# Two spectral layers and two Mish MLPs on one core: the transposed turn through memory, one pipeline step fewer, the ordered filter kept early

## The chip, the cores and the metric

One core of one Trainium2 chip runs the whole program in one launch. The metric is device time in microseconds (us). The kernel before took 1103.34 us, the median of three runs (1102.86 to 1104.55). The profile comes from one further execution of it.

## The reference

An activation `x` of 2048 rows by 1024 columns in bf16 passes through four layers, each with a residual sum and a layer norm without gain ahead of it. Layers A filter in the two-dimensional frequency domain; layers B are a dense MLP with the Mish activation. The same weights serve both rounds.

```python
def _A_ref(x, w_r, w_i):                       # spectral layer
    X = rfft2(x.astype(float32), axes=(-2, -1))
    X = X * (w_r + 1j * w_i)                   # 2048 x 513 complex filter
    return irfft2(X, s=(2048, 1024)).astype(bfloat16)
def _B_ref(x, w1, b1, w2):                     # 1024 -> 3584 -> 1024
    h = x @ w1 + b1
    sp = log1p(exp(-abs(h))) + where(h > 0, h, 0)
    return (h * tanh(sp)) @ w2
x = x + _A_ref(_layernorm(x), w_r, w_i);  x = x + _B_ref(_layernorm(x), w1, b1, w2)
x = x + _A_ref(_layernorm(x), w_r, w_i);  x = x + _B_ref(_layernorm(x), w1, b1, w2)
```

## The kernel before

`x` stays in on-chip memory (`XS`, 16 row tiles `j` of 128 rows). Every engine has one list of instructions that is written out in program order, and the helper classes add the semaphore waits; the order on an engine is thus the order of the code. Three lists can issue DMAs: SP, ACT and POOL.

**Spectral layer (`layer_A`, `li` is 0 or 1).** The transform is split into small dense transforms. `XR` holds the layer's input turned so that a partition is a pair (row tile `j`, 128-column block `h`); `s1` multiplies it by a 128x128 table, in 16 groups of 8 matmuls. In the first layer that table is scaled by the layer norm's factor for each of the 128 columns (`scaled`), on ScalarE for some of every eight and on VectorE for the others. In the second layer the normalised rows come from layer B: fifteen tiles by way of memory (`xn_store`, `xr_load`), the last one directly, one DMA for each of its eight blocks (`xr_direct`).

After `s1` the frequencies are worked through in eight groups `g`, as a software pipeline. One step of the loop takes `s2` of group `g2`, `s3` (forward transform and the product with the filter, four VectorE operations for each half) of `g3`, `i1` of `g4` and `i2` of `g5` (the inverse transforms). Before the change these are the groups `step`, `step - 1`, `step - 3` and `step - 4`, so `i1` comes two steps after its `s3`. Each stage goes TensorE to PSUM, then ScalarE or VectorE copies the PSUM pair away; the four pairs of PSUM banks are used in turn.

The result `u` of a group (16 components by 128 positions in each of 128 partitions) has to be turned so that a component becomes a partition of `UT`. For the groups 0 to 5 this goes through memory: `u_turn` writes `u` to a scratch tensor (512 KB) and `u_back` reads it into 16 rows of `UT`. For the groups 6 and 7, at the end of the pipeline, each component is one on-chip DMA of 32 KB into one partition (`row`; 32 of them over the SP, POOL and ACT lists). When all of `UT` is there, `i4` multiplies it back and layer B begins.

**The filter.** The weights have to be put into the pipeline's order of frequencies: `filter_bins` does this with 12 small matmuls, two VectorE copies and two ScalarE copies for a group. In layer A of `li` 0 it runs inside the pipeline, one group a step, into a ring `WT` of four groups. For `li` 1 the ordered filter is read from a scratch tensor `w_scratch`. Before the change `keep_filter` makes that tensor during the first layer B: it loads the weights once more, orders them once more and stores them, one group after each of eight pairs of matmul blocks.

**Layer B.** `i4` and the residual sum, layer norm, transposes, then `mm1` (to 3584, Mish on ScalarE) and `mm2` (back to 1024), for four chunks `c` of 512 rows. The chunks 2 and 3 run `mm1` one after the other for each of 14 weight blocks `fg`; that is the loop that `keep_filter` sits in. In the profile `mm1` is L933, `mm2` L951, `i4` L878, the filter's matmuls L836, and every DMA L242.

Of the kernel before, what the change touches and what calls it, by code (L numbers as in the profile page):

```python
# [7 lines left out]
P = 128  # L8
# [108 lines left out]
    return (0, 8) if g == 0 else (g, 16 - g)  # L117


def make_tables():  # L120
    n2, dh = np.arange(16.0), np.arange(8.0)
    reps = [None] * P
    for g in range(8):
        a, b = slots_of(g)
# [6 lines left out]
    M = np.zeros((16, 8, P))  # L131
# [6 lines left out]
    half = np.arange(64.0)  # L138
# [16 lines left out]
    FT, BT = [], []  # L155
# [9 lines left out]
    return dict(M0=M.reshape(P, P), M=M.transpose(1, 0, 2).reshape(P, P), MT=M.reshape(P, P).T, JT=np.concatenate([J, -J, J0, -J0], axis=1),  # L165
                FD=np.concatenate(FD, axis=1), BD=np.concatenate(BD, axis=1), FT=by_group(FT), BT=by_group(BT),
                ident=np.eye(P))

# [6 lines left out]
class KB:  # L175
# [176 lines left out]
    def layout(self):  # L352
        K = 1024
        self.o = dict(XR=0, Z=0, X=12 * K, T=20 * K, YK=28 * K, V=40 * K, JT=48 * K, M0=49 * K, IDF=49 * K + 256, RT=50 * K,
                      JUNK=51 * K, WR=54 * K, YS=56 * K, UT=64 * K, MN=64 * K, Y=96 * K, XN=128 * K, U=128 * K,
                      FT=140 * K, BT=144 * K + 512, WT=self.W1_OFF, WR2=140 * K, WT2=144 * K, JT2=148 * K)
# [142 lines left out]

    def pair(self):  # L500
# [39 lines left out]
    def scaled(self, j):  # L540
        rt = self.RT
        rc = rt.ap.rearrange("p a b -> p (a b)")
        for q in range(8):
            n = 8 * j + q
            if q % 3 == 2:
                self.op(self.act, lambda e, n=n: e.activation(self.MN.ap[:, n, :], self.M0.ap, ACT.Copy, scale=rc[:, n:n + 1]),
                        reads=[rt.res, self.M0.res], parts=[self.r_mn[j]])
            else:
                self.op(self.dve, lambda e, n=n: e.tensor_scalar(self.MN.ap[:, n, :], self.M0.ap, rc[:, n:n + 1], None, op0=ALU.mult),
                        reads=[rt.res, self.M0.res], parts=[self.r_mn[j]])  # L550
# [49 lines left out]
    def load_btabs(self, g):  # L600
        b = self.BTr[g % 3]
        self.dma(self.pool, b.ap, self.con["BT"][g], f"bt{g % 3}", writes=[b.res])

    def load_w(self, g):
        if self.li == 0:
            self.load_wr(self.WR[g % 2], g)
            return
        i = 2 * g % 8
        off = (self.o["WT"] + 2048 * i) // 2
        ap = self.ARENA[:, off:off + 2048].rearrange("p (a b c) -> p a b c", a=2, b=2)  # L610
        self.dma(self.pool, ap, self.w_d[g], f"wt{g % 4}", reads=[self.r_wd[g]], writes=[w.res for w in self.WT[i:i + 2]])

    def layer_A(self, li):
        if li == 0:
# [146 lines left out]
        def row(prog, g, r):  # L761
            u = U[g % 3]
            self.dma(prog, self.UT.ap[r * 8 + g:r * 8 + g + 1, :, :], u.ap[:, r, :], f"u{prog.name}{g % 3}",
                     reads=[u.res], parts=[self.UT.res])
# [22 lines left out]
        U = ring("U", 3, 4 * K, [16, P])  # L787
        self.UT = self.alloc("UT", o["UT"], [P, P])
        self.UT.res.begin()
        for step in range(8 + 4):  # L790
            g2, g3, g4, g5 = step, step - 1, step - 3, step - 4
            for h in range(2):
                if 0 <= g2 < 8:
                    s2(g2, h)
                if 0 <= g2 < 8 and h == 0 and li == 0:
                    filter_bins(g2)
                if 0 <= g3 < 8:
                    s3(g3, h)
                if 0 <= g4 < 8:
                    i1(g4, h)  # L800
                if 0 <= g5 < 8:
                    i2(g5, h)
                    u_turn(g5, h)
            if 0 <= g3 < 8 and g3 + 2 < 8:
                load_tabs(g3 + 2)
            if li == 0 and g2 + 2 < 8:
                load_w(g2 + 2)
            if li and 1 <= g2 < 5:
                load_w(g2 + 3)
            if 0 <= g4 < 8 and g4 + 2 < 8:  # L810
                load_btabs(g4 + 2)
            if 0 <= g5 - 1 < 6:
                u_back(g5 - 1)
# [39 lines left out]

    def keep_filter(self, g):

        o = self.o
        if g == 0:
            jt = self.alloc("JT2", o["JT2"], [4 * P])
            self.dma(self.pool, jt.ap, self.con["JT"], "jt2", reads=[self.UT.res], writes=[jt.res])
            self.kf = (jt, self.alloc("WR2", o["WR2"], [2, 2, 512]),  # L860
                       [self.alloc(f"WS{i}", o["WT2"] + 2048 * i, [2, 512]) for i in range(2)])
            self.load_wr(self.kf[1], 0)
        jt, wr, ws = self.kf
        self.filter_bins(g, self.PS[:, 6:8, :].rearrange("p a b -> p (a b)"), self.r_bank[6:8], wr, ws, o["WT2"], jt.ap, jt.res, self.dve)
        ap = self.ARENA[:, o["WT2"] // 2:o["WT2"] // 2 + 2048].rearrange("p (a b c) -> p a b c", a=2, b=2)
# [32 lines left out]
    def layer_B(self, li, last):  # L898
# [203 lines left out]
```

## Time and profile before

| what | us |
|---|---|
| median of the runs | 1103.34 |
| the profiled execution | 1102.66 |
| its span from first to last instruction | 1100.8 |
| TensorE busy in it | 985.6 |
| VectorE busy | 377.1 |
| ScalarE busy | 333.4 |
| GpSimd busy | 81.0 |

The first layer A runs from the start to about 140 us of the span, the first layer B to about 575, the second layer A to about 678, the second layer B to the end. Times inside the span are counted from its start. What the profile calls POOL is GpSimd, and SPq, POOLq and ACTq are DMA issues on those engines' lists. The granted clock is the share of full speed that the TensorE throttle gave; a group's "idle" in brackets is the time that its engine stood still before it, and the name behind the arrow is what ended that.

### The profile page before, as it was taken

The numbers are of one execution on the slowest core, as the hardware profiler recorded it, in microseconds if no ns is written. First come the engines' busy times: TensorE is split into PE (matmuls) and PEld (weight loads), VectorE is DVE, ScalarE is ACT, GpSimd is POOL, SyncE is SP. The second block draws the span as 40 slices with busy tenths as digits, with TensorE's granted clock in tenths as the row PEclk, the third lists the DMA queues.
The fourth block names the chain that finished last, engine by engine and source line by source line (L and its number), as shares of the span: only waits on it lengthen the run. The fifth ranks groups of instructions, "written<-read, shape, count | busy, mean of one in ns | idle before, by whom it ended". The sixth has DMA issues, their size and how long they took to land. (4 is left out here: it accounts for less than half of the span.)

```text
span 1100.8 us, 14504 instructions
## 1 busy us (share of the span) xinstructions
PE 985.6 (90%) x6185; PEld 521.0 (47%) x6185; DVE 377.1 (34%) x843; ACT 333.4 (30%) x466; POOL 81.0 (7%) x129
## 2 busy tenths in 40 slices
PE   0699469999999999999985992899999999999998
PEld 0577344444444445444434772444444444444443
DVE  7977473700444201013343883635011110000111
ACT  6688343332000244310004871433300003331000
POOL 1031200000000022110410211000000000000000
PEclk9699779999999999999997995799999999999999
DMA  9655942444000155320762589034420002210000
GB/s 288 136 145 159 164 124 77 149 149 142 20 20 20 58 172 172 134 76 21 95 89 18 174 197 151 18 126 143 153 86 20 20 29 77 77 39 10 20 20 29
DMA packets 137439, 105.05 MB, mean 95 GB/s; under 512 B 57728, under 2 KB 115328, under 8 KB 137376
## 3 DMA queue, kind: packets, MB, share of 16 engines
q1 hardware_dynamic: 125776, 75.65, 25.0%
q0 software_dynamic: 10016, 28.12, 10.7%
q10 hardware_dynamic: 1584, 0.36, 0.6%
q8 instruction: 49, 0.80, 0.3%
q14 instruction: 14, 0.11, 0.0%
HBM read 83.07 MB, written 18.61 MB: 92 GB/s over the span
## 5 line engine op out<-in xcount | busy, mean ns | idle before, releaser
L933 PE MATMUL PS<-ARENA 128*128 128x512 bf16 x1792 | 392.3, 380 | 3.0 <-DVE ARENA L920 1.6
L951 PE MATMUL PS<-ARENA 128*128 128x512 bf16 x1792 | 390.0, 379 | 0.0
L937 ACT ACTIVATE ARENA<-PS,B 128x512 bf16<-128x512 f32 x224 | 153.7, 687 | 437.0 <-PE PS L933 436.9
L933 PEld LDWEIGHTS PS<-ARENA 128*128 128x128 bf16 x1792 | 175.0, 98 | 211.7 <-issue 2.2
L951 PEld LDWEIGHTS PS<-ARENA 128*128 128x128 bf16 x1792 | 174.7, 98 | 207.7
L956 DVE TENSOR_TENSOR XS<-PS,XS 128x512 bf16<-128x512 f32 x64 | 44.3, 691 | 500.4 <-PE PS L951 500.4
L431 DVE BATCH_NORM_STATS2 BN<-XS 128x6 f32<-128x512 bf16 x108 | 69.5, 673 | 7.7 <-DMA XS<-in_A_x_dram 6.5
L878 PE MATMUL PS<-MT,ARENA 128*128 128x32 bf16 (+1 forms) x768 | 24.5, 186 | 44.0 <-DMA ARENA<-ARENA 35.7
L884 DVE TENSOR_TENSOR XS<-PS,XS 128x512 bf16<-128x512 f32 (+1 forms) x40 | 29.1, 789 | 83.9 <-PE PS L878 83.9
L570 ACT ACTIVATE ARENA<-PS 128x1024 bf16<-128x1024 f32 x16 | 16.2, 1022 | 119.9 <-PE PS L564 119.6
L847 DVE COPY ARENA<-ARENA 128x1024 bf16<-128x1024 bf16 (+1 forms) x32 | 21.9, 730 | 69.6 <-DMA ARENA<-in_A_w_i_dram 61.9
L878 PEld LDWEIGHTS PS<-MT,ARENA 128*128 128x128 bf16 x768 | 22.8, 100 | 47.5 <-issue 40.0
L412 ACT ACTIVATE ARENA<-XS 128x1024 bf16<-128x1024 bf16 x20 | 21.1, 1057 | 62.5 <-DVE XS L884 51.4
L643 PE MATMUL PS<-FD,ARENA 128*128 128x256 bf16 (+1 forms) x312 | 33.7, 258 | 2.4 <-DVE ARENA L572 2.4
L688 ACT ACTIVATE ARENA<-PS 128x1024 bf16<-128x1024 f32 x32 | 33.0, 1032 | 9.4 <-PE PS L684 7.6
L717 ACT ACTIVATE ARENA<-PS 128x1024 bf16<-128x1024 f32 x32 | 33.0, 1031 | 5.4 <-PE PS L710 5.4
L710 PE MATMUL PS<-ARENA 128*128 128x256 bf16 x256 | 34.1, 277 | 0.0
L692 DVE TENSOR_TENSOR ARENA<-ARENA 128x1024 bf16<-128x1024 bf16 x32 | 22.1, 689 | 25.8 <-ACT ARENA L688 20.5
L643 PEld LDWEIGHTS PS<-FD,ARENA 128*128 128x128 bf16 x312 | 26.6, 100 | 8.0 <-DVE ARENA L572 2.9
L915 PE MATMUL PS<-IDENT,ARENA 128*128 128x128 bf16 x256 | 21.4, 241 | 9.6 <-DVE ARENA L474 7.1
L710 PEld LDWEIGHTS PS<-ARENA 128*128 128x128 bf16 x256 | 25.1, 99 | 8.9 <-issue 0.3
L836 PE MATMUL PS<-ARENA 128*128 128x64 bf16 x192 | 24.8, 293 | 4.1 <-DMA ARENA<-in_A_w_i_dram 3.1
(67 smaller groups left out, 584.1 us busy)
## 6 DMA issues: line engine op xcount, KB each, us to landing
ARENA<-in_B_w_dram SPq DMA_DIRECT2D x56, 512.0 KB, 4.0
ARENA<-in_B_w_dram SPq DMA_DIRECT2D x56, 256.0 KB, 4.4
u_scratch<-ARENA SPq DMA_DIRECT2D x12, 512.0 KB, 3.2
ARENA<-u_scratch SPq DMA_DIRECT2D x12, 512.0 KB, 5.3
XS<-in_A_x_dram SPq DMA_DIRECT2D x4, 1024.0 KB, 8.9
ARENA<-in_A_x_dram SPq DMA_DIRECT2D x32, 128.0 KB, 3.3
ARENA<-in_A_w_r_dram POOLq DMA_DIRECT2D x16, 256.0 KB, 4.2
ARENA<-in_A_w_i_dram POOLq DMA_DIRECT2D x16, 256.0 KB, 4.3
```

Source lines behind the costliest of these rows:

```text
L431: self.op(self.dve, lambda e: e.bn_stats(self.BN[:, j, 6 * h:6 * h + 6], self.XS[:, j, 512 * h:512 * h + 512]), reads=[self.r_xs[j]], part ...
L643: fns.append(lambda e: e.matmul(dst, at(r), FD[:, t:t + dst.shape[-1] * 2], start=start, stop=stop))
L688: self.op(act, lambda e: e.activation(x.ap.rearrange("p a b -> p (a b)"), ps, ACT.Copy, scale=SIG), reads=banks, writes=[x.res])
L710: fns.append(lambda e, c=c, part=part: e.matmul(ps[:, c * 256:(c + 1) * 256], yk.ap[:, part, c * P:(c + 1) * P], t[:, (128, 0)[part]:(384, ...
L717: self.op(act, lambda e: e.activation(v.ap[:, :, i, :], src, ACT.Copy), reads=banks, parts=[v.res])
L836: fns.append(lambda e, col=col, j=(j0 + c) * P, mov=mov: e.matmul(ps[:, col:col + 64], jt[:, j:j + P], mov, start=True, stop=True))
L878: fns.append(lambda e, l=l: e.matmul(ps[:, w * l:w * l + w], self.UT.ap[:, u0 + l, :], self.MT[:, 8 * lo:8 * lo + w], start=True, stop=True))
L884: self.op(self.dve, lambda e: e.tensor_tensor(xs, src, xs, ALU.add), reads=rb, parts=self.r_xs[lo:lo + nb])
L933: fns.append(lambda e, db=db, bank=bank, fl=fl: e.matmul(PS[:, bank, :], wb.ap[:, db, fl * P:(fl + 1) * P], x.ap[:, db, :], start=(db == 0 ...
L937: self.op(act, lambda e, bank=bank, ft=ft: e.activation(at.ap[:, ft, :], PS[:, bank, :], ACT.Mish, bias=self.B1[:, ft:ft + 1]), reads=[sel ...
L951: fns.append(lambda e, i=i, ft=ft: e.matmul(PS[:, bank, :], at.ap[:, ft, t * P:(t + 1) * P], W2[ft].ap[:, h * 512:(h + 1) * 512], start=(i ...
L956: self.op(dve, lambda e: e.tensor_tensor(xs, PS[:, bank, :], xs, ALU.add), reads=[self.r_bank[bank]], writes=[self.r_xs[j]])
```

## The change

There are five edits.

1. `u_turn` sends the groups 6 and 7 through memory as well. Group 7 is written in two halves as its halves become ready; the read of group 6 is issued between the two. Group 7 is read back in two halves of the positions, one on SP's list and one on ACT's. The 32 one-partition DMAs of each spectral layer are gone.
2. `i1` now follows its `s3` by one step, and `i2` follows `i1` by one as before; the loop has 11 steps where it had 12.
3. `keep_filter` stores each group of the ordered filter from the `WT` ring in the first spectral layer, one step after `filter_bins` made it, on POOL's list. The eight orderings in layer B, their weight loads and their buffers are gone.
4. The rows of `XR` in the second layer are placed by `row_of(j, h)`: row tile `j` takes eight partitions four apart inside one quarter of the 128, where it took eight partitions sixteen apart. The table `M` is permuted to suit.
5. In `scaled`, ScalarE takes three of every eight tables (it took two), VectorE five.

```diff
+def row_of(j, h):
+    return j % 4 + 4 * h + 32 * (j // 4)
...
-        self.dma(self.pool, self.XR.ap[j:P:16, :, :], self.xn_d[j].rearrange("n (h l) -> h n l", l=P), f"xl{j % 4}",
+        self.dma(self.pool, self.XR.ap[row_of(j, 0):row_of(j, 7) + 1:4, :, :], self.xn_d[j].rearrange("n (h l) -> h n l", l=P), f"xl{j % 4}",
...
-            self.dma(prog, self.XR.ap[16 * h + j:16 * h + j + 1, :, :], b.ap[:, h * P:(h + 1) * P], "xd" + prog.name,
+            self.dma(prog, self.XR.ap[row_of(j, h):row_of(j, h) + 1, :, :], b.ap[:, h * P:(h + 1) * P], "xd" + prog.name,
...
-            if q % 3 == 2:
+            if q % 3 == 1:
...
         def u_turn(g, half):
             u = U[g % 3]
-            if g < 6:
-                if half:
-                    self.dma(sp, self.u_d[g], u.ap, f"uw{g % 3}", reads=[u.res], writes=[self.r_ud[g]])
-                return
-            order = {6: ((sp, pool) * 4,) * 2, 7: ((sp, pool) * 4, (act, sp, pool, act, sp, act, sp, act))}
-            for i in range(8):
-                row(order[g][half][i], g, 8 * half + i)
+            if g == 7:
+                h = slice(8 * half, 8 * half + 8)
+                if half == 0:
+                    self.r_ud[g].begin()
+                self.dma(sp, self.u_d[g][:, h, :], u.ap[:, h, :], f"uwh{half}", reads=[u.res], parts=[self.r_ud[g]])
+            elif half:
+                self.dma(sp, self.u_d[g], u.ap, f"uw{g % 3}", reads=[u.res], writes=[self.r_ud[g]])
+            if g and (half == 0) == (g == 7):
+                u_back(g - 1)
+            if g == 7 and half:
+                u_back(7)
         def u_back(g):
-            self.dma(sp, self.UT.ap[g:P:8, :, :], self.u_d[g].rearrange("l r n -> r l n"), f"um{g % 3}",
-                     reads=[self.r_ud[g]], parts=[self.UT.res])
+            for i, prog in enumerate((sp, act) if g == 7 else (sp,)):
+                l = slice(64 * i, 64 * i + 64) if g == 7 else slice(0, P)
+                self.dma(prog, self.UT.ap[g:P:8, l, :], self.u_d[g][l].rearrange("l r n -> r l n"), f"u{prog.name}{g % 3}",
+                         reads=[self.r_ud[g]], parts=[self.UT.res])
...
-        for step in range(8 + 4):
-            g2, g3, g4, g5 = step, step - 1, step - 3, step - 4
+        for step in range(8 + 3):
+            g2, g3, g4, g5 = step, step - 1, step - 2, step - 3
...
+            if li == 0 and 1 <= g2 < 9:
+                self.keep_filter(g2 - 1)
...
     def keep_filter(self, g):
-        self.filter_bins(g, self.PS[:, 6:8, :].rearrange("p a b -> p (a b)"), self.r_bank[6:8], wr, ws, o["WT2"], jt.ap, jt.res, self.dve)
-        self.dma(self.pool, self.w_d[g], ap, "ws", reads=[w.res for w in ws], writes=[self.r_wd[g]])
-        if g < 7:
-            self.load_wr(wr, g + 1)
+        i = 2 * g % 8
+        self.dma(self.pool, self.w_d[g], self.wt_pair(i), f"ws{g % 4}", reads=[w.res for w in self.WT[i:i + 2]], writes=[self.r_wd[g]])
...
             mm1(2, fg)
             mm1(3, fg)
-            if not last and 2 <= fg < 10:
-                self.keep_filter(fg - 2)
```

Three places show how the instructions now stand. The first is SP's list at the end of the first spectral layer, before: `u_scratch<-ARENA` is the write of a group's `u`, `ARENA<-u_scratch` its way back into `UT`, `ARENA<-ARENA` a one-partition row of the groups 6 and 7, `in_B_w_dram` the weights of layer B.

```order
L242 DMA u_scratch<-ARENA 128x2048
L242 DMA ARENA<-u_scratch 16x128x128
L242 DMA ARENA<-ARENA 1x128x128 x8
L242 DMA ARENA<-u_scratch 16x128x128
L242 DMA ARENA<-ARENA 1x128x128 x7
L242 DMA ARENA<-in_B_w_dram 128x8x256 x4
```

And now, from the write of group 6 on:

```order
L247 DMA u_scratch<-ARENA 128x2048
L247 DMA ARENA<-u_scratch 16x128x128
L247 DMA u_scratch<-ARENA 128x1024
L247 DMA ARENA<-u_scratch 16x128x128
L247 DMA u_scratch<-ARENA 128x1024
L247 DMA ARENA<-u_scratch 16x64x128
L247 DMA ARENA<-in_B_w_dram 128x8x256 x4
```

Fifteen rows have become a write and a read for group 6, and two half writes and a half read for group 7; the read of group 6 stands between the two half writes. The other half read is on ACT's list.

The second place is TensorE's list in the third step of the first spectral layer (`s2` is L643, the filter L836, `s3` L681 to L684), before:

```order
L643 MATMUL PS<-FD,ARENA 128x2x128 x8
L836 MATMUL PS<-ARENA 128x64 x12
L681 MATMUL PS<-ARENA 128x512
L682 MATMUL PS<-ARENA 128x512
L683 MATMUL PS<-ARENA 128x512
L684 MATMUL PS<-ARENA 128x512
L643 MATMUL PS<-FD,ARENA 128x2x128 x2
```

The same step now, where L717 is `i1` and the `s3` lines are L688 to L691:

```order
L650 MATMUL PS<-FD,ARENA 128x2x128 x8
L844 MATMUL PS<-ARENA 128x64 x12
L688 MATMUL PS<-ARENA 128x512
L689 MATMUL PS<-ARENA 128x512
L690 MATMUL PS<-ARENA 128x512
L691 MATMUL PS<-ARENA 128x512
L717 MATMUL PS<-ARENA 128x256 x8
L650 MATMUL PS<-FD,ARENA 128x2x128 x2
```

The first `i1` has moved one step forward, between the `s3` and the second half of `s2`.

The third place is TensorE's list in the first layer B, where the chunks 2 and 3 run `mm1`, before:

```order
L951 MATMUL PS<-ARENA 128x512 x28
L933 MATMUL PS<-ARENA 128x512 x96
L836 MATMUL PS<-ARENA 128x64 x12
L933 MATMUL PS<-ARENA 128x512 x32
L836 MATMUL PS<-ARENA 128x64 x12
L933 MATMUL PS<-ARENA 128x512 x32
```

And now, with `mm1` at L930, `mm2` at L948 and the transposes ahead of it at L912:

```order
L948 MATMUL PS<-ARENA 128x512 x56
L912 MATMUL PS<-IDENT,ARENA 128x128 x8
L948 MATMUL PS<-ARENA 128x512 x28
L930 MATMUL PS<-ARENA 128x512 x448
L948 MATMUL PS<-ARENA 128x512 x448
```

Eight groups of twelve small matmuls are gone, and 448 matmuls of `mm1` stand in one piece.

More of the change, by code (lines that the diff above doesn't have):

```diff
@@ L164, in make_tables @@
     J0 = np.roll(np.eye(P)[::-1], 1, axis=1)
-    return dict(M0=M.reshape(P, P), M=M.transpose(1, 0, 2).reshape(P, P), MT=M.reshape(P, P).T, JT=np.concatenate([J, -J, J0, -J0], axis=1),
+    return dict(M0=M.reshape(P, P), M=M.reshape(P, P)[np.argsort([row_of(j, h) for j in range(16) for h in range(8)])], MT=M.reshape(P, P).T, JT=np.concatenate([J, -J, J0, -J0], axis=1),
                 FD=np.concatenate(FD, axis=1), BD=np.concatenate(BD, axis=1), FT=by_group(FT), BT=by_group(BT),
@@ L355, in layout @@
                       JUNK=51 * K, WR=54 * K, YS=56 * K, UT=64 * K, MN=64 * K, Y=96 * K, XN=128 * K, U=128 * K,
-                      FT=140 * K, BT=144 * K + 512, WT=self.W1_OFF, WR2=140 * K, WT2=144 * K, JT2=148 * K)
+                      FT=140 * K, BT=144 * K + 512, WT=self.W1_OFF)
         self.ob = dict(AT0=0, AT1=36 * K, XT1=28 * K, XT0=120 * K, W2=64 * K)
@@ L602, in load_btabs, with wt_pair @@
         self.dma(self.pool, b.ap, self.con["BT"][g], f"bt{g % 3}", writes=[b.res])
+    def wt_pair(self, i):
+        off = (self.o["WT"] + 2048 * i) // 2
+        return self.ARENA[:, off:off + 2048].rearrange("p (a b c) -> p a b c", a=2, b=2)
     def load_w(self, g):
@@ L608, in load_w @@
         i = 2 * g % 8
-        off = (self.o["WT"] + 2048 * i) // 2
-        ap = self.ARENA[:, off:off + 2048].rearrange("p (a b c) -> p a b c", a=2, b=2)
-        self.dma(self.pool, ap, self.w_d[g], f"wt{g % 4}", reads=[self.r_wd[g]], writes=[w.res for w in self.WT[i:i + 2]])
+        self.dma(self.pool, self.wt_pair(i), self.w_d[g], f"wt{g % 4}", reads=[self.r_wd[g]], writes=[w.res for w in self.WT[i:i + 2]])
     def layer_A(self, li):
@@ L854, in keep_filter @@
     def keep_filter(self, g):
[L856 to L863, printed above, removed]
-        self.filter_bins(g, self.PS[:, 6:8, :].rearrange("p a b -> p (a b)"), self.r_bank[6:8], wr, ws, o["WT2"], jt.ap, jt.res, self.dve)
-        ap = self.ARENA[:, o["WT2"] // 2:o["WT2"] // 2 + 2048].rearrange("p (a b c) -> p a b c", a=2, b=2)
-        self.dma(self.pool, self.w_d[g], ap, "ws", reads=[w.res for w in ws], writes=[self.r_wd[g]])
-        if g < 7:
-            self.load_wr(wr, g + 1)
+        i = 2 * g % 8
+        self.dma(self.pool, self.w_d[g], self.wt_pair(i), f"ws{g % 4}", reads=[w.res for w in self.WT[i:i + 2]], writes=[self.r_wd[g]])
     def i4(self, lo, nb, u0, n, bank, staged=None):
```

6 lines of the change are left out of this document (removed).

## The prediction

> **What bounds the kernel now.** I read the page's busy shares first, then what TensorE waits for, then the timelines around its longest waits.
>
> ```profile
> PE 985.6 (90%) x6185; PEld 521.0 (47%) x6185; DVE 377.1 (34%) x843; ACT 333.4 (30%) x466; POOL 81.0 (7%) x129
> ```
>
> TensorE is the bound on average, so a gain is either matmuls taken out or a TensorE wait shortened. The list of its waits (total, times, longest) names the second kind:
>
> ```profile
> PE PS L878 <- DMA ARENA<-ARENA: 35.7, 2, 18.5
> PE PS L564 <- DMA ARENA<-ARENA: 13.2, 1, 13.2
> PE PS L564 <- DVE ARENA L549: 6.6, 6, 1.6
> PE PS L836 <- DMA ARENA<-in_A_w_i_dram: 3.1, 7, 0.9
> PE PS L681 <- DVE ARENA L673: 1.1, 1, 1.1
> PE PS L836 <- DVE ARENA L673: 0.9, 1, 0.9
> ```
>
> The first row is the turn into `UT` at the end of both spectral layers, the second the last row tile on its way into `XR`, the third the scaled tables of the first `s1`. The fourth stands in the first layer B. The last two are small stalls early in the two pipelines.
>
> **The filter out of layer B (edit 3).** TensorE's timeline there, and the chain of waits for the same 448 matmuls in the second layer B, which has no filter:
>
> ```profile
> 365.74 20.88 PE L933 MATMUL PS<-ARENA 128*128 128x512 bf16 x96
> 386.46 1.55 PE L836 MATMUL PS<-ARENA 128*128 128x64 bf16 x12
> 387.84 7.09 PE L933 MATMUL PS<-ARENA 128*128 128x512 bf16 x32
> 395.25 1.55 PE L836 MATMUL PS<-ARENA 128*128 128x64 bf16 x12 [0.33 <-DMA ARENA<-in_A_w_i_dram]
> ...
> 450.19 27.81 PE L933 MATMUL PS<-ARENA 128*128 128x512 bf16 x128
> 477.83 2.54 PE L951 MATMUL PS<-ARENA 128*128 128x512 bf16 x11
> 904.26 96.69 PE PS L933 x448
> 1000.95 96.71 PE PS L951 x448
> ```
>
> With the filter the stretch takes 477.83 - 365.74 = 112.09 us, without it 96.69: 15.4 us, all of it on TensorE's own path. It can be counted from below too: 386.46 to 387.84 is 1.38 for one group, eight are 11.0, and the waits for the weight loads add 3.1, 14.1 together; the rest is lost around each change-over. I take **-15.4** (14.1 to 15.6). The VectorE and ScalarE copies that go with it were beside matmuls and count nothing, and neither do the sixteen weight loads.
>
> The stores move into the first spectral layer. What they meet there:
>
> ```profile
> 60.00:110.00 50.00, 49.06 (x437) 38.18 (x435) 40.88 (x73) 42.50 (x52) 11.62 (x19) 0.97 0.52 148
> 389.87 0.57 POOL L242 DMA_DIRECT2D w_scratch<-ARENA  x1 [183.32 <-ACT ARENA L851]
> w_scratch<-ARENA POOLq DMA_DIRECT2D x8, 512.0 KB, 3.0
> ```
>
> The columns of the first are the stretch, its length, busy time of PE, PEld, DVE, ACT and POOL, granted clock, DMA share and GB/s. TensorE is busy 49.06 of 50, the DMA engines 0.52 of the time, POOL's list is mostly idle. Eight issues of 0.57 us go past POOL's loads of weights and tables, which are asked for a step or more ahead; eight transfers, at most 3.0 us each from issue to landing, over some 70 us put the DMA share near 0.8. `filter_bins` of group `g + 4` must now also wait for the store of `g`, asked for three steps earlier. I cost it at **0**, hidden under TensorE; if that cover is gone it is one landing, up to +3.
>
> **The turn at the end of a spectral layer (edit 1).** VectorE's last copies of `u`, three in a row, and TensorE's first matmul on `UT`, in both layers; then issue to landing of each kind of transfer, in the quiet pipeline (first two) and in the busy ends (next three):
>
> ```profile
> 120.74 3.52 DVE L757 CAST ARENA<-PS 128x1024 bf16<-128x1024 f32 x3 [0.64 <-PE PS L749]
> 140.05 4.79 PE L878 MATMUL PS<-MT,ARENA 128*128 128x32 bf16 x178 [17.19 <-DMA ARENA<-ARENA]
> 657.57 3.60 DVE L757 CAST ARENA<-PS 128x1024 bf16<-128x1024 f32 x3 [0.64 <-PE PS L749]
> 678.29 1.89 PE L878 MATMUL PS<-MT,ARENA 128*128 128x32 bf16 x65 [18.52 <-DMA ARENA<-ARENA]
> u_scratch<-ARENA SPq DMA_DIRECT2D x6, 512.0 KB, 3.2
> ARENA<-u_scratch SPq DMA_DIRECT2D x5, 512.0 KB, 5.2
> u_scratch<-ARENA SPq DMA_DIRECT2D x1, 512.0 KB, 4.1
> ARENA<-u_scratch SPq DMA_DIRECT2D x3, 512.0 KB, 7.7
> ARENA<-u_scratch SPq DMA_DIRECT2D x3, 512.0 KB, 10.4
> 655.47 0.54 SPq L242 DMA_DIRECT2D ARENA<-u_scratch  x1
> ```
>
> Call the end of the last copy C: 124.26 and 661.17. `UT` is usable at C + 15.8 and C + 17.1. After the change the path is a chain on SP's list: group 6 is written when its second copy ends, two copies (2.35) ahead of C; its read waits for that landing; the second half of group 7, though ready at C, is queued behind that waiting read; then it lands, and group 7 is read back. By quiet rows: -2.35 + 3.2 + 0.54 + 3.2 + 5.2 = C + 9.8. By busy rows, 4.1 and 7.7: C + 14.1. The two layers together gain 13.3 by the quiet rows and 4.7 by the busy ones. The transfers are smaller at the end (halves), but a write and a read of 512 KB for each step leave the queue full, so I take the middle, **-9.0** for both. Splitting the last read over two lists saves one issue, 0.54 at most. ACT's half waits ahead of the next layer norm's work, which needs `UT` anyhow.
>
> The Trainium skill speaks against this detour. Its page "DMA: Bandwidth & Descriptors", section "Anatomy of one DMA — SWDGE (gpsimd) path", gives each DMA a fixed cost of about 2.0 us, most of it the receipt of the last byte and longest for HBM, plus bytes over 436 GB/s. By that page, as an estimate, 1 MB straight across lands after 4.4 us, and a write and a read of 256 KB in turn take 5.2: the detour would be 0.8 us slower in each layer. The row with 17.19 disagrees with the first half: 32 one-row DMAs took over 15 us. Whether the second half holds is a rival below.
>
> **One step less (edit 2).** Steps hold the same work, so only waits can change. `s3` ends on TensorE, and VectorE ends its product:
>
> ```profile
> 613.01 0.38 PE L684 MATMUL PS<-ARENA 128*128 128x512 bf16 x1
> 617.74 0.42 DVE L699 TENSOR_TENSOR ARENA<-ARENA 128x512 bf16<-128x512 bf16 x1
> 620.37 0.38 PE L684 MATMUL PS<-ARENA 128*128 128x512 bf16 x1
> ```
>
> This is the largest lag that I found, 5.2 us; the next step's `s3` of that half, behind which `i1` now stands, is at 620.37, 7.4 us after the first. So `i1` finds its data 2.2 us early at the worst. The two early stalls (1.1 and 0.9) should go, because `i1` gives TensorE work while VectorE catches up. At the end it turns round: in the last full step VectorE has two `u` copies of 1.2 us more, and the product of the last half may come about a microsecond late, in each layer. Net **-0.5** (from -2.0 to +2.5).
>
> **Rows of `XR` (edit 4).** The last tile is normalised at 578.51, its first matmul waits until 587.84; below are TensorE, VectorE, and issue to landing:
>
> ```profile
> 577.96 0.55 DVE L474 TENSOR_SCALAR ARENA<-XS,RS 128x1024 bf16<-128x1024 bf16 x1
> 587.84 10.66 PE L564 MATMUL PS<-M,ARENA 128*128 128x128 bf16 x128 [13.15 <-DMA ARENA<-ARENA]
> ARENA<-ARENA SPq DMA_DIRECT2D x3, 32.0 KB, 6.7
> ARENA<-ARENA ACTq DMA_DIRECT2D x3, 32.0 KB, 7.5
> ```
>
> The eight DMAs stay, with other destinations. If their partitions collided, the landing could fall from 7.5 to the 3.2 of a quiet write: -4.3; if not, 0. The one-row DMAs of the turn go to rows eight apart, another spread, and land no faster:
>
> ```profile
> ARENA<-ARENA SPq DMA_DIRECT2D x15, 32.0 KB, 7.0
> ```
>
> That is the nearest row, so I stay near nothing: **-1.0**. The Trainium skill, "SBUF — State Buffer", section "Door 1: The DMA port swizzle", puts the old rows of a tile on four ports of 27.2 GB/s and the new on eight; by that page 256 KB would take 1.2 us instead of 2.4, an estimate of -1.2, and the sum would be 0.2 lower.
>
> **Scaled tables (edit 5).** Two groups of the first `s1` on both engines:
>
> ```profile
> 39.80 2.03 DVE L549 TENSOR_SCALAR ARENA<-ARENA 128x128 bf16<-128x128 bf16 x12
> 39.88 1.02 ACT L570 ACTIVATE ARENA<-PS 128x1024 bf16<-128x1024 f32 x1 [0.90 <-PE PS L564]
> 40.80 1.26 ACT L546 ACTIVATE ARENA<-ARENA 128x128 bf16<-128x128 bf16 x4
> 41.75 1.22 DVE L572 CAST ARENA<-PS 128x1024 bf16<-128x1024 f32 x1
> ```
>
> VectorE needs 2.03 + 1.22 = 3.25 for two groups, ScalarE 2.28. With ten and six tables it is 1.69 + 1.22 = 2.91 against 1.89 + 1.02 = 2.91. Five such pairs are still to come once the input is there, and they overlap a little: **-0.7** (0 to -1.7).
>
> **Sum.** -15.4 + 0 - 9.0 - 0.5 - 1.0 - 0.7 = -26.6. The profiled execution took 1102.66 (1.9 around its span of 1100.8), 0.7 below the median of the runs; so 1076.1 for it and **1076.7** for the median.
>
> **Rivals.** (a) The detour is no shorter: with the busiest landings, 4.1 and 10.4, the chain ends at C + 16.8, as before. The page's rule on the fixed cost would bring about the same. For it speaks that the queue is full at that place, against it that the 10.4 belongs to a read that shared the engines with 32 row transfers, which are gone. Time 1076.7 + 9 = 1085.7. (b) The chain runs as fast as the quiet rows and the `XR` rows land at 3.2: another 4.3 + 3.3, so 1069. (c) The filter's gain is handed back: the stores push the DMA share of the first spectral layer to its limit, and each step waits about a landing, 3.0, for weights; eight are 24, so 1100.7. The share of 0.52 speaks against. (d) Slower: `i1` comes before its product, in both layers, in all 32 halves. The decision point is a lag above 7.4 us where the trace's largest is 5.2; to end above 1103.34 every `i1` would have to wait 26.6 / 32 = 0.83 us, a lag of 8.2 throughout. Early TensorE time is limited by VectorE, which speaks for it; VectorE, busy 40.88 us of the 50 in the row further up, has time left to catch up, which speaks against. With it 1104 or more.
>
> **How the numbers follow.** My forecast has 0.58, (a) 0.18, (b) 0.16, (c) 0.05, (d) 0.03. A measurement of this kernel tells 0.2%, 2.2 us, from no change. Only (d) and an unlikely (c) reach that: faster 0.95, the same 0.02, slower 0.03. The range takes in (a) and (b) with the open ends of the small terms: 1066 to 1088.
>
> **What would show it.** After the change, `mm1` of chunks 2 and 3 should stand as one piece of 96.7 us in both layers B. The waits for `UT` should be some 13 us each, released by a read from the scratch tensor, and VectorE's last copy should lie within a microsecond of its old distance from the pipeline's start. The wait of the second `s1` should be 12 to 13 us. No wait of L717 on VectorE should exceed a microsecond. The prediction fails if TensorE waits for weights or tables inside the first spectral layer, if the second half write of group 7 lands later than C + 7, or if the 15.4 turns up again in another wait of layer B.

## The result, and the profile after

The changed kernel took 1071.38 us, the median of four runs (1070.27 to 1071.76); the kernel before took 1103.1 beside it. The ratio is 0.971, 95% interval 0.9693 to 0.9727: 31.7 us faster, where 26.6 had been forecast. The time lies inside the predicted range (1066 to 1088), 5.3 below the predicted 1076.7.

The profiled execution has a span of 1068.5, 32.3 shorter than before. Its busy shares:

```profile
PE 973.0 (91%) x6089; PEld 509.6 (48%) x6089; DVE 362.4 (34%) x811; ACT 330.2 (31%) x466; POOL 55.3 (5%) x86
```

TensorE lost 96 matmuls and 12.6 us of work. The rest of the gain is in its waits (total, times, longest):

```profile
PE PS L875 <- DMA ARENA<-u_scratch: 27.9, 2, 14.0
...
PE PS L569 <- DMA ARENA<-ARENA: 11.0, 1, 11.0
...
PE PS L569 <- DVE ARENA L554: 4.1, 4, 1.6
```

The turn is now released by a read from the scratch tensor and waits 27.9 where it waited 35.7; the last row tile costs 11.0 where it cost 13.2; the scaled tables 4.1 where 6.6. No row names a wait of `i1` (L717), and the two early stalls of the pipelines are gone.

TensorE's timeline (start, length, what, wait ahead of it): first `s1` of the first layer, the first `i4`, `mm1` and then `mm2` of chunks 2 and 3, `s1` of the second layer, its first `i4`.

```profile
36.19 1.87 PE L569 MATMUL PS<-ARENA 128*128 128x128 bf16 x16 [0.81 <-DVE ARENA L554]
38.90 1.89 PE L569 MATMUL PS<-ARENA 128*128 128x128 bf16 x16 [0.85 <-DVE ARENA L554]
...
44.42 1.89 PE L569 MATMUL PS<-ARENA 128*128 128x128 bf16 x16 [0.85 <-DVE ARENA L554]
...
131.28 4.86 PE L875 MATMUL PS<-MT,ARENA 128*128 128x32 bf16 x176 [13.99 <-DMA ARENA<-u_scratch]
...
357.07 3.19 PE L930 MATMUL PS<-ARENA 128*128 128x512 bf16 x14
...
453.77 11.60 PE L948 MATMUL PS<-ARENA 128*128 128x512 bf16 x53
...
561.61 10.20 PE L569 MATMUL PS<-M,ARENA 128*128 128x128 bf16 x128 [10.98 <-DMA ARENA<-ARENA]
...
645.92 5.60 PE L875 MATMUL PS<-MT,ARENA 128*128 128x32 bf16 x204 [13.88 <-DMA ARENA<-u_scratch]
```

From such rows the span can be cut at the same events in both kernels. Each number is the difference of two starts or ends in one profile:

| stretch | before | after | difference | forecast |
|---|---|---|---|---|
| start to the first `s2` of layer 1 (tables) | 50.32 | 47.49 | -2.83 | -0.7 |
| from there to the end of VectorE's last `u` copy | 73.94 | 71.36 | -2.58 | step: -0.5 in all |
| from there to the first `i4` (turn) | 15.79 | 12.43 | -3.36 | turn: -9.0 for both |
| `mm1` of chunks 2 and 3 (filter) | 112.09 | 96.70 | -15.39 | -15.4 |
| last row tile normalised to the second `s1` (`XR`) | 9.33 | 7.17 | -2.16 | -1.0 |
| the second `s1` | 11.86 | 11.40 | -0.46 | 0 |
| second pipeline to VectorE's last `u` copy | 61.47 | 60.59 | -0.88 | step, above |
| from there to the first `i4` (turn) | 17.12 | 12.32 | -4.80 | turn, above |

The differences add up to 32.5. The rest (the two layers B outside these stretches) became 0.2 longer, which gives the 32.3 of the span. C below is, as in the prediction, the end of VectorE's last `u` copy.

### The profile page after: what moved, and what is told of

Read it like the earlier page. It is cut to its first block, busy times and chain, and to the rows that moved or that the text cites. A ratio compares the mean times of both kernels' runs of the same rounds, so it can differ in the third digit from the quotient of the medians.

```text
span 1068.5 us, 14145 instructions
## 1 busy us (share of the span) xinstructions
PE 973.0 (91%) x6089; PEld 509.6 (48%) x6089; DVE 362.4 (34%) x811; ACT 330.2 (31%) x466; POOL 55.3 (5%) x86
## 5 line engine op out<-in xcount | busy, mean ns | idle before, releaser
L930 PE MATMUL PS<-ARENA 128*128 128x512 bf16 x1792 | 393.7, 382 | 1.6 <-DVE ARENA L917 1.6
L948 PE MATMUL PS<-ARENA 128*128 128x512 bf16 x1792 | 390.0, 379 | 0.0
L930 PEld LDWEIGHTS PS<-ARENA 128*128 128x128 bf16 x1792 | 175.5, 98 | 214.3 <-issue 6.0
L948 PEld LDWEIGHTS PS<-ARENA 128*128 128x128 bf16 x1792 | 174.5, 98 | 207.8
L875 PE MATMUL PS<-MT,ARENA 128*128 128x32 bf16 (+1 forms) x768 | 24.7, 189 | 36.1 <-DMA ARENA<-u_scratch 27.9
L717 PE MATMUL PS<-ARENA 128*128 128x256 bf16 x256 | 33.2, 273 | 0.1
L717 PEld LDWEIGHTS PS<-ARENA 128*128 128x128 bf16 x256 | 24.6, 98 | 9.7 <-DVE ARENA L706 0.9
L912 PE MATMUL PS<-IDENT,ARENA 128*128 128x128 bf16 x256 | 21.6, 242 | 8.3 <-DVE ARENA L479 5.8
L738 PE MATMUL PS<-ARENA,BD 128*128 128x256 bf16 x192 | 25.9, 273 | 0.4 <-DVE ARENA L764 0.2
L912 PEld LDWEIGHTS PS<-IDENT,ARENA 128*128 128x128 bf16 x256 | 18.6, 109 | 14.0 <-DVE ARENA L479 6.9
```

Of the source, the lines that this page charges most:

```text
L717: fns.append(lambda e, c=c, part=part: e.matmul(ps[:, c * 256:(c + 1) * 256], yk.ap[:, part, c * P:(c + 1) * P], t[:, (128, 0)[part]:(384, ...
L875: fns.append(lambda e, l=l: e.matmul(ps[:, w * l:w * l + w], self.UT.ap[:, u0 + l, :], self.MT[:, 8 * lo:8 * lo + w], start=True, stop=True))
L912: fns.append(lambda e, db=db: e.transpose(PSb[:, bank, db * P:(db + 1) * P], xn.ap[:, db * P:(db + 1) * P], self.IDENT[:]))
L930: fns.append(lambda e, db=db, bank=bank, fl=fl: e.matmul(PS[:, bank, :], wb.ap[:, db, fl * P:(fl + 1) * P], x.ap[:, db, :], start=(db == 0 ...
L948: fns.append(lambda e, i=i, ft=ft: e.matmul(PS[:, bank, :], at.ap[:, ft, t * P:(t + 1) * P], W2[ft].ap[:, h * 512:(h + 1) * 512], start=(i ...
```

## The experiments

Each is timed against the kernel before on the same chip, in alternation. A ratio is turned into microseconds with 1103.3. The stretches below are those of the table.

**Each edit alone: the filter.** The kernel before, with edit 3 and nothing else:

```diff
+            if li == 0 and 1 <= g2 < 9: self.keep_filter(g2 - 1)   # store from the ring
-            if not last and 2 <= fg < 10: self.keep_filter(fg - 2) # load and order again
```

> The kernel before with edit 3 alone (filter stored in the first spectral layer). Theory: mm1 of chunks 2 and 3 stands in one piece of 96.7 us, the first spectral layer is as long as before (73.9 us from first s2 to last copy), 15.4 us less in all. Rival: the stores delay loads or the turn in the first spectral layer, and some of it is given back: 12 to 14 less.

Measured: ratio 0.9844 (0.9828 to 0.986), so 17.2 us. `mm1` of chunks 2 and 3 takes exactly 96.70. The first pipeline is 73.78, as before (73.94), so the stores cost nothing there. The row of -15.4 is right. Among the five profiles that still order the filter in layer B (before, and the other edits alone), that stretch lies between 110.9 and 114.5, so in other executions it gives back 14 to 18; the profile before is the second lowest of them. The two longest (114.5 with the turn alone, 114.1 with the step alone) are those in which TensorE waits 1.30 and 1.53 for a weight load of the filter, and in both the granted clock then falls to 0.50 for a few microseconds; in the three others the longest such wait is 0.5 to 1.1, and no such fall follows.

**The turn alone.** Edit 1 in the kernel before:

```diff
-            order = {6: ((sp, pool) * 4,) * 2, 7: (...)}       # 32 one-partition DMAs
+            if g == 7: ...  # two half writes, the read of group 6 between them, two half reads
```

> The kernel before with edit 1 alone (groups 6 and 7 through memory). Theory: the turns take 12.4 and 12.3 us after VectorE's last copy, as in the changed kernel, instead of 15.8 and 17.1: 8.2 less. Rival: the gain hangs on the shorter pipeline, whose last steps leave the transfers more time; with the old steps the queue is fuller and the gain is 5 or less.

Measured: 0.9887 (0.9869 to 0.9905), 12.5 us. Its two turns are 11.81 and 12.32 long, which is the middle of the predicted C + 9.8 to C + 14.1. The gain is larger than the 8.2 of the two profiles, in part because of the kernel before: in the four profiles with the old steps that turn groups 6 and 7 by rows, the turns last 15.8 to 17.2 and 16.0 to 18.1, 33.8 together in the mean, and against that mean the gain is 9.7. The profile that I predicted from has the shortest of the first. What the timed runs gained beyond 9.7 is not explained.

**The step alone.** Edit 2 in the kernel before:

```diff
-        for step in range(8 + 4):
-            g2, g3, g4, g5 = step, step - 1, step - 3, step - 4
+        for step in range(8 + 3):
+            g2, g3, g4, g5 = step, step - 1, step - 2, step - 3
```

> The kernel before with edit 2 alone (one step less). Theory: the edits work each in their own stage, and the shorter pipeline itself takes away the early stall of TensorE and the 4 us of half clock that follow it in the first spectral layer: from first s2 to the last copy 71.4 us instead of 73.9 there and 60.6 instead of 61.5 in the second, 3.5 us less in all, the turns into UT unchanged (15.8 and 17.1). Rival: the half clock after the stall is an accident of the profiled execution or comes from the other edits; then the first pipeline stays above 73 and the time falls by 1.5 or less.

Measured: 0.9992 (0.9981 to 1.0003): nothing. Both pipelines are shorter (72.52 and 60.58, against 73.94 and 61.47), the first by less than expected. Both turns, which I had expected unchanged, are longer (18.88 and 18.44, against 15.79 and 17.12; the three other profiles with rows and the old steps have up to 17.2 and 18.1). VectorE's and SP's rows of this kernel at the end of the first pipeline:

```profile
116.60 5.97 DVE L757 CAST ARENA<-PS 128x1024 bf16<-128x1024 f32 x5
...
118.98 6.41 SPq L242 DMA_DIRECT2D ARENA<-ARENA  x8
125.43 0.62 SPq L242 DMA_DIRECT2D ARENA<-u_scratch  x1
126.10 12.40 SPq L242 DMA_DIRECT2D ARENA<-ARENA  x7
```

VectorE has five `u` copies left in one run of 5.97, where before the last run had three (3.52). So two groups are handed to the DMAs in a burst. The issue of the last seven rows takes 12.40, where it took 10.28 before. I read this as row transfers that are bound by their own rate, with a list that is full; no run varies that rate alone, so this is argued and not shown.

**The rows of `XR` alone.** Edit 4 in the kernel before:

```diff
-    XR.ap[j:P:16]
+    XR.ap[row_of(j, 0):row_of(j, 7) + 1:4]        # and M permuted
```

> The kernel before with edit 4 alone (rows of XR). Theory: the eight direct transfers of the last tile land sooner because their rows no longer share ports; the stretch from the last tile's normalisation to the second s1 falls from 9.3 to 7.1 us, 2.2 less in all, and the landings from 6.7 and 7.5 to some 4.4 and 5.3. Rival: the placing does nothing and the shorter wait came with the other edits; then 9.3 us stay and the time is the same within 0.5 us.

Measured: 0.9979 (0.9965 to 0.9993), 2.3 us; the stretch is 7.32 against 9.33. Issue to landing of the one-row DMAs, in this kernel and then in the changed one:

```profile
ARENA<-ARENA SPq DMA_DIRECT2D x3, 32.0 KB, 4.7
ARENA<-ARENA ACTq DMA_DIRECT2D x3, 32.0 KB, 5.5
```

```profile
ARENA<-ARENA SPq DMA_DIRECT2D x3, 32.0 KB, 4.4
ARENA<-ARENA ACTq DMA_DIRECT2D x3, 32.0 KB, 5.3
```

They were 6.7 and 7.5. Nothing but the partitions that they write to has changed, so those partitions set about 2 us of the landing. The loads of the other fifteen tiles, placed in the same way, gain too: from issue to landing 7.7 in this kernel and 11.7 before.

**All of a tile's rows close together.** The changed kernel with the opposite placement: a tile's eight rows in two blocks of four neighbouring partitions, 32 apart. A tile's load from memory thereby becomes two DMAs of four rows each.

```diff
 def row_of(j, h):
-    return j % 4 + 4 * h + 32 * (j // 4)
+    return 4 * (j % 8) + 64 * (j // 8) + h % 4 + 32 * (h // 4)
```

> The changed kernel with the eight rows of an input tile put on partitions 4p to 4p + 3 and 32 above them, which by the Trainium skill's page SBUF, section Door 1, all share one port of 27.2 GB/s; a tile's load from memory becomes two transfers. Theory: ports limit the direct transfers; 256 KB through one port take 9.6 us by that page plus what is fixed, so the stretch from the last tile to the second s1 grows from 7.2 to 11 us or more. Rival: the placing matters in another way or not at all; the stretch stays between 7 and 9.5.

Measured: 1155.21 us, 1.0452 (1.0437 to 1.0468). The direction was right, the size far off. The wait of the second `s1`, and four of POOL's loads of tiles from memory in this kernel:

```profile
PE PS L570 <- DMA ARENA<-ARENA: 93.3, 1, 93.3
```

```profile
563.09 2.17 POOL L247 DMA_DIRECT2D ARENA<-xn_scratch  x2 [11.89 <-issue]
...
572.37 2.17 POOL L247 DMA_DIRECT2D ARENA<-xn_scratch  x2 [7.11 <-issue]
...
581.96 2.18 POOL L247 DMA_DIRECT2D ARENA<-xn_scratch  x2 [7.42 <-issue]
...
592.04 2.17 POOL L247 DMA_DIRECT2D ARENA<-xn_scratch  x2 [7.90 <-issue]
```

The loads go 9.3 to 10.1 us apart, 256 KB each: 26 to 28 GB/s. I had thought of the last tile only; but the tiles that come by way of memory are placed in the same fashion, and they queue up one after the other until the last tile stands behind all of them. The Trainium skill, "SBUF — State Buffer", section "Door 1: The DMA port swizzle", puts these eight rows on one port of 27.2 GB/s; this run agrees in place and rate. It does not tell a port from mere neighbourhood of the partitions, and no run cuts the loads in two without moving them. By the map of the Trainium skill's same section the rows of `UT` that a group is read back to lie on eight ports, 218 GB/s as an estimate. There the traces disagree: the kernel before, in quarters of a microsecond from 648 to 658 us, while such reads run (648.5 to 649.75 and 654 to 655.25), holds some 290; the higher figures stand where `u` is written:

```profile
GB/s 246 124 287 291 292 292 285 239 202 153 0 0 0 0 0 0 246 459 377 246 246 279 213 107 278 291 289 292 290 260 202 277 338 311 393 311 262 213 87 258
```

**The scaled tables alone.** Edit 5 in the kernel before:

```diff
-            if q % 3 == 2:
+            if q % 3 == 1:        # ScalarE: three of eight
```

> The kernel before with edit 5 alone (three of eight scaled tables on ScalarE). Theory: VectorE set the pace of the first s1, the two engines are now even, and the first s2 starts at 47.5 us instead of 50.3: 2.8 less in all. Rival: the earlier start came with the other edits, or what is gained is lost to the input loads: 0.7 or less.

Measured: 0.9935 (0.992 to 0.995), 7.2 us. Its stretch gained 2.8 (47.54 against 50.32), and so did it in every kernel with this edit (47.4 to 47.6). The other 4.4 stand in no stretch that the edit touches. Between the two profiles the span differs by 3.5 only (1100.8 to 1097.3). The kernel before had a median of 1105.36 in this round, 2.3 above the 1103.1 beside the changed kernel, and ranged from 1101.75 to 1107.34 over all runs, where the changed kernel stayed within 1070.27 to 1071.76. So some of the 4.4 may lie in the kernel before; no run settles it. How the 2.8 comes about is in TensorE's timeline of the kernel before, beside the rows of after shown above:

```profile
40.91 2.01 PE L564 MATMUL PS<-ARENA 128*128 128x128 bf16 x16 [1.07 <-DVE ARENA L549]
44.00 2.01 PE L564 MATMUL PS<-ARENA 128*128 128x128 bf16 x16 [1.07 <-DVE ARENA L549]
47.08 2.01 PE L564 MATMUL PS<-ARENA 128*128 128x128 bf16 x16 [1.07 <-DVE ARENA L549]
```

Two groups came every 3.085 us (40.91 to 47.08 in two steps) and now come every 2.743 (36.19 to 44.42 in three), 0.34 less. VectorE sets this pace from the first to the last of the eight pairs: 8 x 0.34 = 2.7.

**The changed kernel without edit 2.**

```diff
+        for step in range(8 + 4):
+            g2, g3, g4, g5 = step, step - 1, step - 3, step - 4
```

> The changed kernel with edit 2 undone (i1 two steps after s3 again). Theory: alone, edit 2 shortened the two pipelines by 2.3 us and lost as much in the turns made of one-row transfers, which are bound by their own rate; with the turn through memory the gain stays. Then this kernel is 3 us slower than the changed one, with the stall of 0.9 us and mostly the half clock after it back in the first pipeline (73.3 to 74.3 us) and turns of 11.8 and 12.3. Rival: edit 2 gains nothing in company either; same time as the changed kernel within 1 us.

Measured: 1071.71, 0.9699 (0.9685 to 0.9713), not the 3 us more that I expected: the changed kernel, run again in another round, took 1071.13, 0.970 (0.968 to 0.9719). With the turn through memory too, edit 2 is worth nothing that can be measured. Its pipelines are 73.74 and 61.47 (2.4 and 0.9 longer than after), its turns 11.47 and 11.78 (1.0 and 0.5 shorter).

**The stores twice.** The changed kernel; each group of the ordered filter goes to a second scratch tensor as well.

```diff
         self.dma(self.pool, self.w_d[g], self.wt_pair(i), f"ws{g % 4}", ...)
+        self.dma(self.pool, self.w2_d[g], self.wt_pair(i), f"wx{g % 4}", ...)
```

> The changed kernel with every group of the ordered filter stored twice in the first spectral layer (4 MB more written from POOL's list). Theory: the stores are hidden under TensorE with room to spare; the first pipeline stays between 71 and 72.5 us, the turn after it near 12.4, the same time. Rival: the transfers are near their limit there, and 4 MB more push weights, tables or the turn back: 3 us or more in the first spectral layer.

Measured: 1070.94, 0.9698 (0.9678 to 0.9717). The first pipeline in windows (busy times of PE, PEld, DVE, ACT, POOL, granted clock, DMA share, GB/s), here and in the changed kernel:

```profile
47.50:119.00 71.50, 69.94 (x660) 55.26 (x660) 55.31 (x91) 57.68 (x69) 25.88 (x41) 0.97 0.86 277
```

```profile
47.50:119.00 71.50, 69.66 (x660) 55.00 (x660) 55.43 (x91) 57.61 (x69) 19.77 (x33) 0.98 0.72 219
```

Another 4 MB raises the DMA share from 0.72 to 0.86, and TensorE is as busy as before. The share of 0.72 is below the 0.8 of the prediction. Rival (c) is refuted with room to spare.

**The half writes on another list.** Where do the turn's 12.4 us go? SP's list and ACT's one entry at the end of the first pipeline of the changed kernel, and the landings there:

```profile
116.61 0.46 SPq L247 DMA_DIRECT2D u_scratch<-ARENA  x1
117.26 0.54 SPq L247 DMA_DIRECT2D ARENA<-u_scratch  x1
117.84 2.82 SPq L247 DMA_DIRECT2D u_scratch<-ARENA  x1
120.94 0.54 SPq L247 DMA_DIRECT2D ARENA<-u_scratch  x1
121.53 2.03 SPq L247 DMA_DIRECT2D u_scratch<-ARENA  x1
126.68 0.55 SPq L247 DMA_DIRECT2D ARENA<-u_scratch  x1
...
126.67 0.64 ACTq L247 DMA_DIRECT2D ARENA<-u_scratch  x1
```

```profile
u_scratch<-ARENA SPq DMA_DIRECT2D x2, 256.0 KB, 5.5
ARENA<-u_scratch ACTq DMA_DIRECT2D x1, 256.0 KB, 4.3
ARENA<-u_scratch SPq DMA_DIRECT2D x1, 256.0 KB, 3.4
```

The rows of SP are, in order: write of group 6, read of 5, first half of 7, read of 6, second half of 7, first half read of 7. VectorE's last copy ends at C = 118.85, but the second half write is issued only from 121.53 to 123.56, and its read begins at 126.68. Two things keep this write back. It stands behind the read of 6, which waits for the write of 6 and is issued at 120.94, and its issue, which takes 0.3 to 0.6 for the writes ahead of it, then takes 2.03 (2.82 for the first half): the list is blocked, which I had not counted. So both half writes go to ACT's list:

```diff
-                self.dma(sp, self.u_d[g][:, h, :], u.ap[:, h, :], ...)
+                self.dma(act, self.u_d[g][:, h, :], u.ap[:, h, :], ...)
```

> The changed kernel with both half writes of group 7 issued from ACT's list instead of SP's. Theory: in the changed kernel the second half write stands behind the waiting read of group 6 and behind its packets, which leaves the transfers idle for about 2.5 us before the last read; on a queue of its own it lands earlier, the last read follows without the gap, and each turn falls from 12.4 to about 10.2 us: 4.4 less than the changed kernel. Rival: only the place behind the read counts, and the turn falls to the quiet chain of 9.8 or below, 7 less. Second rival: the transfers are the limit and the read of group 6 is put off by as much as the write gains: no difference.

Measured: 1066.34, 0.9649 (0.9635 to 0.9663), about 5 us better than the changed kernel. VectorE, ACT's list and TensorE of this kernel, and the landing of its half writes:

```profile
113.34 5.96 DVE L764 CAST ARENA<-PS 128x1024 bf16<-128x1024 f32 x5
...
118.21 1.46 ACTq L247 DMA_DIRECT2D u_scratch<-ARENA  x2
124.71 0.65 ACTq L247 DMA_DIRECT2D ARENA<-u_scratch  x1
...
129.84 4.85 PE L875 MATMUL PS<-MT,ARENA 128*128 128x32 bf16 x176 [12.09 <-DMA ARENA<-u_scratch]
...
u_scratch<-ARENA ACTq DMA_DIRECT2D x2, 256.0 KB, 5.2
```

C is 119.30 here. Both writes are out by 119.67, the last read starts at C + 5.4 where it was C + 7.8, and the turn is 10.54 (10.29 in the second layer). From the start of its issue to its landing a half write takes 5.2, hardly less than the 5.5 on SP's list. So, as far as this shows, the blocked issue as such cost little; what was gained is the start of the second half, at C instead of C + 2.7, behind nobody's wait. Only 3.9 of the 5 stand in the two turns.

**The last copies on two engines.** The five copies of VectorE in one run of 5.97 are next. On top of the half writes on ACT's list, ScalarE takes the copies of the second halves of groups 5 and 6 and of the first half of group 7; the line is the condition for VectorE:

```diff
-                    if g > 4 or (half == 0 and g % 2 and li):
+                    if (g > 4 and half == (g == 7)) or (g < 5 and half == 0 and g % 2 and li):
```

> The changed kernel with both half writes of group 7 on ACT's list, and with the last six copies of u shared between VectorE and ScalarE (group 5 and 6: first half VectorE, second half ScalarE; group 7 the other way round) instead of all on VectorE. Theory: the shorter pipeline's gain is lost at its end because five copies of 1.2 us stand one behind the other on VectorE while ScalarE is idle; shared, the writes of groups 5 and 6 start some 1.5 us earlier and the last copy ends about 1 us earlier, in both layers; with the half writes on ACT (4 us) some 6 to 7 us less than the changed kernel. Rival: the transfers at the end are the limit, and only the 4 us of the half writes are seen.

> The kernel with the half writes on ACT and the shared copies, but edit 2 undone. Theory: once VectorE's copies no longer hold up the end, edit 2 is worth its shorter pipelines, 3 us in all, so this one is 3 us slower than the kernel with shared copies. Rival: edit 2 is worth nothing here either, within 1 us.

Measured: 1065.33, 0.9651 (0.9629 to 0.9673). The turns are 9.41 and 9.70. This is the fastest kernel of the study by its median, 5.8 below the changed kernel run beside it, but its ratio can't be told from that of the half writes on ACT's list. With edit 2 undone in it: 1068.45, 0.9678 (0.9658 to 0.9699), turns 9.91 and 10.64, pipelines 74.13 and 61.35 against 71.99 and 60.30. By the medians edit 2 is worth some 3 us once the burst at the end is spread; the intervals of the two ratios overlap, though each of the five runs with the old steps (1068.04 and more) is slower than each of the four beside them (1067.92 and less). So this is likely, but the ratios do not show it.

The changed kernel run again beside these three, as their base line:

> The changed kernel once more, beside the others of this call, for their differences to it. Both theories: 0.971 of the time before, turns of 12.3 to 12.5 us.

Measured: 1071.13, 0.970 (0.968 to 0.9719), turns of 12.64 and 12.38.

## Why the prediction was right or wrong

- **Filter, -15.4:** right. -15.39 in its stretch, in company and alone, and its stores cost nothing even when they are doubled.
- **Turn, -9.0:** right in size, -8.2 in the profiles, C + 12.4 and C + 12.3 between the quiet and the busy end. The order on SP's list sets a part of it, 1.9 and 2.0, as the run with the half writes on ACT's list shows. The second half did stand behind the waiting read. Two terms of the chain were off against each other: the half write took 5.5 from the start of its issue, blocked issue included, instead of 3.2 to 4.1, so the second half was in memory at C + 7.8, past the C + 7 that I had named as a sign of failure; and the last reads of 256 KB took only 3.4 and 4.3, against 5.2 to 7.7 for 512 KB. That the two errors cancel is luck. Rival (a) falls. The Trainium skill, "DMA: Bandwidth & Descriptors", section "Anatomy of one DMA — SWDGE (gpsimd) path", had spoken against this term: by the estimate in the prediction the detour would be 0.8 slower in each layer. The turns disagree (15.8 to 18.1 by rows with the old steps, 12.3 and 12.4 through memory). That section is on transfers which GpSimd issues, and the detour's are issued by SP and ACT.
- **One step less, -0.5:** right in the sum of the timed runs (0.9 alone, some 0.6 in company, both within the noise), but for partly other reasons, so the sum is luck. The pipelines became shorter by more than I said (2.6 and 0.9), and the last copy moved by more than the microsecond that I allowed. What I had as the product of the last half coming about a microsecond late is a run of five copies, which hands two groups to the DMAs at once; the turn gives back 0.5 to 1.0 in each layer, and with the row transfers, against the kernel before, 1.3 to 3.1. Rival (d) is refuted: `i1` waits for nothing.
- **Rows of `XR`, -1.0:** mis-sized, -2.2. I took the row transfers of the turn as the nearest row, which showed no gain from another spread, and they were a poor guide. Those stand 32 deep in the lists and here there are eight; that this is the reason is likely and not shown. The gain is also more than the 1.2 of the estimate beside it. The landings (4.4 and 5.3) are still above the quiet 3.2 of rival (b). The wait in the list is 11.0, below the 12 to 13 that I gave.
- **Scaled tables, -0.7:** mis-sized, -2.8. The 0.34 for a pair was right. I counted five pairs and took off some overlap, but VectorE sets the pace of all eight pairs, and each shrinks by the full 0.34.
- **The sum:** -26.6 forecast, -32.3 between the profiles. The missing 5.7 are the tables (2.1), the pipelines (3.0 net of the 0.5), `XR` (1.2) and the second `s1` (0.5, which is between 10.8 and 12.0 in the kernels whatever the edit), less the turn (0.8). The time lies nearer to the 1069 of rival (b) than to the forecast, but (b) is not what happened: the turns are 12.4 and 12.3 and not 9.8.
- **What stays open:** the edits alone add up to 40 us by their ratios, 8 more than together. Of that, 4.4 are what the kernel with the tables alone gained outside their stretch, and some 4 what the turn alone gained beyond the 8.2; a part lies in the kernel before, whose turns and filter vary, and for the rest no run gives a cause.

## What to carry to other kernels

A transfer that is ready but stands behind another one's wait in the same list costs the whole of that wait (2.7 us here): count the order of the issues, and put the last writes on a list that is idle. When a pipeline is made one step shorter, look at what its last step then does at once, since the work that was spread over two steps comes as a burst to an engine and then to the DMAs. And take several executions of the kernel before where a term rests on one wait: the two turns that I priced varied by 1.4 and 2.1 us between four profiles that share their code.

## What the runs showed of the hardware

The first is the clock. Early in the first pipeline TensorE stands still for 0.9 us (the sixth row of the first list of waits), and this is followed by a stretch at half clock. The windows of 2 us (busy time of PE, granted clock, DMA share, GB/s) of the kernel before, of the changed kernel, and of the fastest one with the old steps:

```profile
72.00:74.00 2.00, 1.18 (x11) 1.00 0.97 283
74.00:76.00 2.00, 2.00 (x11) 0.69 0.36 139
76.00:78.00 2.00, 2.00 (x12) 0.50 0.07 18
78.00:80.00 2.00, 2.00 (x20) 0.96 0.98 233
```

```profile
69.00:71.00 2.00, 2.00 (x20) 1.00 0.96 320
71.00:73.00 2.00, 2.00 (x24) 1.00 0.94 341
```

```profile
69.00:71.00 2.00, 1.07 (x10) 1.00 0.91 270
71.00:73.00 2.00, 2.00 (x14) 0.88 0.94 355
73.00:75.00 2.00, 2.00 (x12) 0.50 0.24 90
75.00:77.00 2.00, 2.00 (x19) 0.77 0.84 195
```

At half clock TensorE does 12 matmuls in 2 us instead of 20 to 24, for some 3.4 us. This happens in six of the seven profiles with the old order of steps and in none of the seven with the new one, where `i1` fills the gap: an effect of edit 2 that the prediction lacked. It is not all of the shorter pipeline: the one kernel with the old order and no dip (`XR` rows alone) takes 73.32, the others of that order 73.74 to 74.30, the seven of the new order 71.4 to 72.6. The Trainium skill, "TensorE: Matmul & The Clock Gate", section "Part 1: The HAM clock gate (the "warmup" mystery)", has the clock drop after an idle window of about 3.4 us. The traces show that length for the slow stretch, but differ on what goes before it: TensorE had been idle for 0.9 us, and for 1.30 and 1.53 in the two falls inside the filter's stretch. An idle of that length does not always bring it on, since the profile of the `XR` rows alone has 0.95 at the same place and no dip; what decides stays open.

The second is that an issue can block: 2.0 and 2.8 us instead of 0.3 to 0.6 on SP while reads of `u` are still under way there, and 12.40 for seven one-row transfers. Without the block, on ACT's list, the landing comes only 0.3 sooner (5.2 against 5.5). The third is how much the partitions matter to which a small transfer goes: 256 KB in eight pieces landed 2 us earlier on partitions four apart than on partitions sixteen apart, and a tile took 9 to 10 us on two blocks of four neighbours.
